# A fused long convolution and maxout feed-forward: where a hand-ordered kernel places its copies, folds and table loads

## The chip, the cores and the metric

The kernel runs on one core of a Trainium2 chip. The metric is the device time of one execution in microseconds (us), and the median over several executions is what is compared. Before the change it is 2282.52 us over 3 runs (2280.43 to 2288.77).

## The reference

A gated long convolution (batch 4, length 12544, 128 channels) feeds a maxout feed-forward layer (768 hidden units). Cut to what matters:

```python
h = (np.maximum(pos_emb @ w1, 0.0) @ w2) * np.exp(-0.01 * pos)[:, None]
u = x * v
y = irfft(rfft(u, n=2*S, axis=1) * rfft(h, n=2*S, axis=0)[None], n=2*S, axis=1)[:, :S]
t = (x * y).reshape(B * S, D)
out = np.maximum(np.maximum(t @ moe_w1, t @ moe_w2), t @ moe_w3) @ moe_w_out
```

All numbers are 32-bit floats.

## The kernel before

**Stages.** The transforms are done as matmuls on TensorE, in two steps: a first step of short transforms per block of four channels (a "unit" `u`, 32 per batch), and a second step per pair `g` of frequencies (45 pairs, `NK`). The filter's own transform and the whole convolution of batch 0 come first ("direct" stage, loop over `s` at L1072). After them comes a "passage" (L1106 to L1172), and then the main stage: for each batch the feed-forward runs over 32 tiles of 392 columns, and beside it, in the gaps that the feed-forward leaves on the other engines, the convolution of the next batch. The last batch's tiles have nothing beside them.

**Order.** The order of all instructions is written out by hand (L147); each engine takes its instructions in that order, and the waits between engines follow from the tiles. A tile in PSUM or SBUF is waited for as a whole. A pool with `bufs=2` gives out two buffers in turn, and the third request waits for the release of the first.

**The direct stage.** Step `s` multiplies pair `s` by the filter's second transform (`s_second`), forms the filter's spectrum of pair `s-1` (`s_filter`, copied to `ht` by ScalarE, L1050), and runs the inverse of pair `s-3` (`g_third`, L570, copied to `zs` by ScalarE and stored to `zd` in DRAM by SP). For pair `s-2` it stores `ht` to `hd` in DRAM from GpSimd's queue (`s_store`, L1054; later batches read it back), takes the complex product on VectorE (`g_re`, `g_im`: three instructions of about 0.69 us) and unfolds the result (`g_unfold`, two of 0.42). At step `NK` the pairs 43 and 44 are both due. At the steps `NK` and `NK + 1` stand units 0 and 1 of batch 1.

**A unit.** `u_first` (L404) does half a unit at a time: 16 matmuls (L413) into a PSUM bank, a copy `high` of one half of the result by ScalarE (L423), and a sum and a difference on VectorE into `spec` (L425). Its input `uT` is the transposed product x*v. Units up to 5 of batch 1 (`EARLY`) are transposed on TensorE (`u_turn`, L368). All later ones go another way: loads by SP (`u_load`), the product on GpSimd (`u_mul`, L361), a copy into two planes of 16-bit halves on ScalarE (`u_planes`, L382), a transposing DMA from SP (`u_dma`, L388), and `u_join` (L392), which puts the halves together again in two copies, L397: one on ScalarE, one on VectorE.

**The passage.** The third weight matrix times the output matrix is folded into one matrix `lin`: six times a transpose (L1007), a copy `w1t` on ScalarE (L1009) and a product accumulated in the bank `pl` (L1010). Units 4 and 5 of batch 1 are transposed between the folds. Then the pools of the first stages are closed. The main stage begins with the loads of two tiles of batch 0 (`t_load`, L675), the sums of the first on VectorE (`t_sums`, L701), unit 2, the tile's last transform (`t_last`, L717: 64 matmuls and a product `gt` on VectorE, L735), the sums of the second, unit 3, and then the loop over the tiles.

**The main loop.** A slot is one sixth of a tile. In each slot `up` (L740) makes two products of 128 hidden units in the banks `hps` (three in turn, L1137); ScalarE takes the first out with a ReLU into `hid` (L745), VectorE takes the maximum with the second (L748). The first eight tiles of a batch go in pairs with seven products instead of eight (`products`, L798), whose sums run on GpSimd (L778) and which need the weight differences `tw` and `linx`: five subtractions, L1190, in the first slots of batch 0.

**What runs beside, and when.** `conv_steps` (L582) plans the next batch's convolution by slot: the units first, then the pairs from slot `s0`. By its formulas `s0` is 55 for batch 1 and 59 for batches 2 and 3. Pairs are started two at a time, about 2.6 slots per pair. For pair `x` SP loads a table (`w_load`, L431, 256 KB, three buffers), for two pairs at a time the spectrum (`q_load`, L437, four transfers of 128 KB, two buffers) and the filter back from `hd` (`h_load`, L451, four transfers of 256 KB, two buffers). The buffers exist from slot `LOADS` = 52 on. SP's queue also carries the tiles' loads (`t_load`, L1198) and, up to that slot, stores of results. `g_quarter` (L462) uses the table and the spectrum in slot `start(x)`, `q_re` uses the filter three slots later or more.

Of the kernel before, what the change touches and what calls it, by code (L numbers as in the profile page):

```python
# [10 lines left out]
FP32 = mybir.dt.float32  # L11
# [5 lines left out]
P = 128  # L17
# [74 lines left out]
def kernel(  # L92
# [299 lines left out]
    def u_join(u):  # L392
        if u % 2 == 0:
            uts[u] = uts[u + 1] = utp.tile([NB, 16, 2, 32], FP32, tag="uT", name="uT")
        t = us.pop(u)
        for h in range(2):
            copies[h](  # L397
                uts[u][:, 8 * (u % 2):8 * (u % 2) + 8].rearrange(
                    "n s r t -> n (s r t)").bitcast(U16).rearrange(
                    "n (s r t h) -> n h s r t", h=2, r=2, t=32)[:, h],  # L400
                t[0:NB, 4 * h:4 * h + 4].rearrange("n s p -> n (s p)").rearrange(
                    "n (s t r) -> n s r t", s=8, r=2))

    def u_first(u, i0=0, n=4):  # L404


        t = uts[u] if i0 + n < 4 else uts.pop(u)
        ps = state["bank"]()[:, 0:256 * n]
        at = 4 * u + i0
        for i in range(n):  # L410
            for h in range(2):
                for c in range(2):
                    nc.tensor.matmul(  # L413
                        ps[64 * c:64 * c + 64, 256 * i + h * N1:256 * i + (h + 1) * N1],
                        t[:, 2 * ((at + i) % 8) + h].rearrange("n r t -> n (r t)"),
                        f1q[:, h, c * N1:(c + 1) * N1],
                        start=(i % 2 == 0 and h == 0), stop=True, skip_group_check=True)
        v = ps.rearrange("p (s m) -> p s m", m=256)[:, :, 0:2 * N1].rearrange(
            "p s (h k) -> p h k s", h=2)
        high = cvp.tile([P, state["eo"]], FP32, tag="eo", name="high", bufs=2)  # L420
        high = high[:].rearrange("p (s k) -> p s k", k=D)[:, 0:n, 0:N1].rearrange(
            "p s k -> p k s")
        nc.scalar.copy(high, v[:, 0])  # L423
        for a, op in enumerate((ALU.add, ALU.subtract)):
            nc.vector.tensor_tensor(out=spec[:, :, a, at:at + n], in0=v[:, 1], in1=high, op=op)  # L425

# [125 lines left out]
    def g_re(g):  # L552
        xt = xts[g]
        nc.vector.tensor_tensor(out=xt[:], in0=xt[:], in1=hts[g][:, 0], op=ALU.mult)
# [27 lines left out]
    def conv_steps(b, done):  # L582


        out = []

        def at(slot, late, fn, *args):
            out.append((slot, late, len(out), fn, args))

        for u in range(4, done):
            at(2 * (u - 4), 1, unit, u)
        lead, low = (1, -NT * NF) if b > 1 else (6, 0)
        share = UNIT * (NU - done - 1)
        per_pair = (END - lead - 6) / (share + (NK + LATE) // 2 * 2 - 2)
        for u in range(done, NU):
            s = (u - done) * UNIT * per_pair + lead
            load_ = max(low, int(s) - 9)
            at(load_, 0, u_load, b, u)  # L600
            mul = max(load_ + 2, int(s) - 6)
            at(mul, 0, u_mul, u, nc.gpsimd)
            at(max(mul, int(s) - 5), 0, u_planes, u)
            at(max(mul + 1, int(s) - 4), 0, u_dma, u)
            at(int(s), 0, u_join, u)
            at(int(s + 1), 1, unit, u)
        s0 = int(share * per_pair + lead) + 6

        def start(x):
            return s0 + int(x // 2 * 2 * per_pair)  # L610

        load = [0.6] * (NT * NF)
        for x in range(NK + LATE):
            s = start(x)
            load[s] -= 1.2
            load[s + 1 + x % 2] += 1.4

        def emptiest(among, cost):
            s = min(among, key=lambda i: load[i])
            load[s] += cost  # L620
            return s

        plan = []
        busy = {start(x): 2 for x in range(NK + LATE)}
        for x in range(NK + LATE):
            busy.setdefault(start(x) + 1, 1)
        for i in range(NT - 1):
            s = i * NF
            last = min((3, 4, 2), key=lambda k: busy.get(s + k, 0))
            load[s + last] += 0.6  # L630
            if s <= s0:
                plan.append((0, 0, last))
                continue
            a = emptiest(range(s, s + 2), 0.7) - s
            plan.append((a, emptiest(range(s + a, s + max(a + 1, last - 1)), 0.7) - s, last))
        plan.append((3, 3, 4))

        for x in range(NK + LATE):
            s, odd = start(x), x % 2
            g, z = x if x < NK else None, x - LATE if x >= LATE else None  # L640
            at(s, 1, g_quarter, g, z)
            at(s + 1 + odd, 0, g_fold, g, z)
            at(max(s - 4, LOADS), 0, w_load, x)
            if z is not None:
                at(s + 3 + odd, 0, g_store, b, z)
            if g is None:
                continue
            if g % 2 == 0:
                at(max(s - 4, LOADS), 0, q_load, g, min(2, NK - g))
                at(s - 1, 0, h_load, g, min(2, NK - g))  # L650
            first = s + 2 + 2 * odd
            at(first, 0, q_swap, g, 0)
            at(first + 1, 0, q_swap, g, 64)
            last = start(x + LATE) - 1
            a = emptiest(range(first + 1, min(first + 3, last - 1) + 1), 0.7)
            at(a, 0, q_re, g)
            a = emptiest(range(a, min(first + 4, last - 1) + 1), 0.7)
            at(a, 0, q_im, g)
            two = sorted(emptiest(range(a + 1, last + 1), 0.55) for _ in range(2))
            for q in range(2):  # L660
                at(two[q], 0, q_unfold, g, q)
        slots = {}
        for s, _, _, fn, args in sorted(out, key=lambda r: r[:3]):
            slots.setdefault(s, []).append((fn, args))
        return slots, plan, s0
# [332 lines left out]
    def bank():  # L998
        return next(free)

    state = {"cv": (cvp, cps), "xb": 2, "bank": bank, "eo": 2 * D,
             "turn": lambda: sps.tile([P, 512], FP32, tag="pl", name="pst")}
    Gs, minus = {}, {}

# [54 lines left out]

    EARLY = 6  # L1060
    loads = dict(zip((NK - 16, NK - 14, NK - 12, NK - 9, NK - 8, NK - 4), range(EARLY)))
    muls = dict(zip((NK - 13, NK - 11, NK - 10, NK - 5, NK - 3, NK - 1), range(EARLY)))
    turns = {NK - 9: 0, NK - 8: 1, NK - 4: 2, NK - 3: 3}
    folded = []

# [6 lines left out]
    for s in range(NK + 3):  # L1072
        if s < NK:
            ws[s, 0] = wf[s]
            s_second(s)
            if s + 1 < NK:
                s_minus(s + 1)
            g_second(s)
            wf.pop(s)
            if s + 3 < NK:  # L1080
                wf[s + 3] = load_dir(s + 3, 0)
        if 1 <= s <= NK:
            g_swap(s - 1)
            s_filter(s - 1)
        if s >= 3:
            ws[s - 3, 1] = wi.pop(s - 3)
            g_third(s - 3)
            if s < NK:
                wi[s] = load_dir(s, 1)
        for g in {NK: (s - 2, s - 1)}.get(s, (s - 2,)):  # L1090
            if 0 <= g < NK and s <= NK:
                s_store(g)
                g_re(g)
                g_im(g)
                g_unfold(g)
        if s < NK:
            g_butterfly(s)

        if s in muls:
            u_mul(muls[s])  # L1100
        if s in turns:
            u_turn(turns[s])
        if s in loads:
            u_load(1, loads[s])
        if s in (NK, NK + 1):
            unit(s - NK)  # L1106
    pl = sps.tile([P, 512], FP32, tag="pl", name="pl")
    state["turn"] = bank
    for f in range(NF):
        folding(f)  # L1110
        if f in (2, 3):
            u_turn(f + 2)
# [14 lines left out]
    b21, b22 = wo_sb[:, NC:, 0:64], wo_sb[:, NC:, 64:128]  # L1127
    weights = [(tw[:, 1], b22, b12), (tw[:, 3], b12, b11), (tw[:, 0], b22, tw[:, 3]),
               (tw[:, 2], b21, tw[:, 0]), (linx[:], lin[:, 0:64], lin[:, 64:128])]
    op_ = ctx.enter_context(tc.tile_pool(name="op", bufs=2))  # L1130
    conv = ExitStack()
    inq = conv.enter_context(tc.tile_pool(name="inq", bufs=1))
# [10 lines left out]
        turn_of["at"] = (turn_of["at"] + 1) % turn_of["of"]  # L1143
        return singles[turn_of["at"]]

    state = {"bank": single, "eo": 4 * D}
    sp = {"hid": ("h11",), "store": nc.sync}


# [9 lines left out]
    for n, (b, i) in enumerate(tiles[:LAST]):  # L1159
# [13 lines left out]
        for f in range(NF):  # L1173
            s = i * NF + f
            turn_ = i == NT - 1
            if i < TP:
# [8 lines left out]
                    down(*late.pop(0))  # L1185
                if n == 0 and f == 0:
                    t_last(tiles[1])
                elif weights:
                    out, a1, a2 = weights.pop(0)
                    nc.vector.tensor_tensor(out=out, in0=a1, in1=a2, op=ALU.subtract)  # L1190
                if j == 0:
                    banks = (obank, singles[3])
                    down_pair(b, i0, h, banks if i0 % 4 == 0 else banks[::-1], s, ends,
# [114 lines left out]
```

## Time and profile before

| what | before |
|---|---|
| median of 3 runs, us | 2282.52 (2280.43 to 2288.77) |
| the profiled execution, us | 2285.45 |
| span in its trace, us | 2283.7 |
| TensorE busy, us (share) | 2248.9 (98%) |
| VectorE busy, us (share) | 1554.7 (68%) |
| ScalarE busy, us (share) | 1264.1 (55%) |
| GpSimd busy, us (share) | 1010.7 (44%) |
| VectorE copies L397, number, mean ns | 90, 1015 |
| ScalarE copies L397, number, mean ns | 90, 777 |
| ScalarE copies `high` L423 from unit 2 of batch 1 on, number, mean ns | 188, 489 |

The names in the profile: PE is TensorE, PEld its weight loads, DVE VectorE, ACT ScalarE, POOL GpSimd, SP SyncE, a q behind a name the queue of that engine; L156 and the like are lines of the kernel, and L156 is that of a helper with which most matmuls are made, so its rows are told apart by their tiles (`hps` hidden units, `ops` output, `cps` with `f4p` a tile's last transform, `ps` with `ab` a pair's inverse). "a <- b" in a list of waits says that a stood idle until b had ended. The direct stage ends near 299 us, the main loop starts near 312, batch 2's convolution begins beside batch 1's tiles at 824, batch 3's near 1345.

### The profile page before, as it was taken

Reading aid. Unit: us, or ns where it says so; the run is one execution under the profiler, and the core shown is the slowest. Engines: PE = TensorE matmul, PEld = TensorE weight load, DVE = VectorE, ACT = ScalarE, POOL = GpSimd, SP = SyncE. Lnnn points to the kernel's source line nnn. Section 1 sums busy time; section 2 is a strip of 40 time slices with the busy share of each in tenths; the row PEclk is TensorE's granted clock in tenths of the full one; section 3 lists DMA queues with packets and bytes.
Section 4 is the critical chain, followed back from the end, with each engine's and each line's share of the span. In section 5 each row is a group of like instructions: output and inputs, shape, how many; then the busy total and the mean of one; then the engine's idle time right before and its main releaser. Section 6 shows DMA issues by size and latency. Waiting matters only on the chain.

```text
span 2283.7 us, 70396 instructions
## 1 busy us (share of the span) xinstructions
PE 2248.9 (98%) x28383; PEld 1427.1 (62%) x28383; DVE 1554.7 (68%) x3016; ACT 1264.1 (55%) x2308; POOL 1010.7 (44%) x1203
## 2 busy tenths in 40 slices
PE   8999989999999999999999999999999999999998
PEld 7988857755555557755555557765555556666665
DVE  5588967657878756658888856658888844544443
ACT  2688856556666656646666646646666622222222
POOL 2044447613333357713333347713333326666666
PEclk9999999999999999999999999999999999999999
DMA  7778989789999789969999889979999832222221
GB/s 187 183 231 269 305 179 179 135 199 248 228 241 234 199 165 186 167 149 250 251 239 233 228 158 182 170 148 254 252 238 232 215 85 56 56 68 67 59 56 22
DMA packets 485569, 411.17 MB, mean 180 GB/s; under 512 B 341305, under 2 KB 387866, under 8 KB 485242
## 3 DMA queue, kind: packets, MB, share of 16 engines
q1 hardware_dynamic: 459778, 334.30, 65.3%
q0 software_dynamic: 24752, 70.65, 10.4%
q8 instruction: 223, 3.65, 0.7%
q10 hardware_dynamic: 712, 1.70, 0.3%
q14 instruction: 104, 0.85, 0.1%
HBM read 262.84 MB, written 84.67 MB: 152 GB/s over the span
## 4 chain that ended last, share of the span: by engine, by line
PE 94%; DMA 3%; DVE 1%; POOL 1%; issue 1%; ACT 1%; SPq 0%; POOLq 0%; ACTq 0%; DVEq 0%
PE hps L156 43%; PE ops L156 14%; PE ops L809 8%; PE cps L413 5%; PE cps L156 4%; PE cps L472 3%; PE ps L156 3%; PE ps L165 3%; PE cps L482 3%; PE cps L809 2%; PE sps L1045 2%; PE gps L1027 1%; PE last L156 1%; DMA hd<-ht 1%; PE pst L366 1%; DMA wt<-wq_const 1%
## 5 line engine op out<-in xcount | busy, mean ns | idle before, releaser
L156 PE MATMUL hps<-gt,w_sb 128*64 128x392 f32 x6144 | 1150.6, 494 | 1.7 <-ACT hid L745 1.7
L745 ACT ACTIVATE hid<-hps 128x392 f32<-128x392 f32 x768 | 382.4, 498 | 665.9 <-PE hps L156 626.1
L156 PEld LDWEIGHTS hps<-gt,w_sb 128*64 128x64 f32 x6144 | 435.8, 137 | 406.0 <-issue 362.7
L748 DVE TENSOR_TENSOR hid<-hid,hps 128x392 f32<-128x392 f32 x768 | 428.5, 558 | 375.6 <-PE hps L156 340.0
L524 POOL TENSOR_TENSOR cb<-cb,xs 128x512 f32<-128x512 f32 x135 | 174.8, 1295 | 457.9 <-DVE xs L521 361.2
L156 PE MATMUL ops<-hid,wo_sb 128*64 128x392 f32 x1728 | 358.4, 492 | 0.0
L497 DVE TENSOR_TENSOR cb<-cps,eo 128x512 f32<-128x512 f32 (+1 forms) x288 | 175.1, 649 | 73.1 <-ACT eo L494 73.1
L156 PEld LDWEIGHTS ops<-hid,wo_sb 128*64 128x64 f32 x1728 | 125.7, 137 | 157.7 <-issue 157.7
L512 ACT ACTIVATE xs<-cb 32x512 f32<-32x512 f32 x270 | 169.5, 628 | 19.6 <-DVE cb L497 10.9
L763 POOL DMA_DIRECT2D out_dram<-ot x72 | 56.8, 789 | 275.4 <-ACT ot L761 223.8
L513 ACT COPY xs<-cb 32x512 f32<-32x512 f32 x270 | 166.3, 616 | 3.1
L425 DVE TENSOR_TENSOR spec<-cps,high 128x180 f32<-128x180 f32 x376 | 110.7, 339 | 69.8 <-ACT high L423 67.5
L423 ACT COPY high<-cps 128x180 f32<-128x180 f32 x188 | 90.9, 489 | 115.7 <-PE cps L413 79.9
L528 DVE TENSOR_TENSOR xs<-cb 128x256 f32<-128x256 f32 x270 | 143.8, 578 | 9.4 <-POOL cb L524 9.4
L413 PE MATMUL cps<-f1q,uT 98*64 98x90 f32 x3008 | 137.2, 243 | 6.3 <-DVE uT L397 5.9
L413 PEld LDWEIGHTS cps<-f1q,uT 98*64 98x64 f32 x3008 | 131.1, 138 | 15.3 <-issue 6.3
L778 POOL TENSOR_TENSOR s<-hid 128x392 f32<-128x392 f32 x84 | 87.2, 1038 | 89.5 <-DVE hid L748 56.1
L505 POOL DMA_DIRECT2D zd<-cb x135 | 92.7, 687 | 63.7 <-DVE cb L497 60.8
L156 PEld LDWEIGHTS cps<-f4p,even 90*64 90x64 f32 x1568 | 91.5, 138 | 30.6 <-issue 28.3
L778 POOL TENSOR_TENSOR s<-hid,s 128x392 f32<-128x392 f32 x84 | 87.3, 1040 | 51.6 <-DVE hid L748 51.3
L361 POOL TENSOR_TENSOR ut<-ut 128x392 f32<-128x392 f32 x90 | 94.9, 1054 | 34.1 <-DMA ut<-in_vr_dram 31.9
L778 POOL TENSOR_TENSOR hid<-hid,s 128x392 f32<-128x392 f32 x84 | 86.5, 1032 | 33.1 <-PE cps L809 9.6
(148 smaller groups left out, 3586.4 us busy)
## 6 DMA issues: line engine op xcount, KB each, us to landing
ht<-hd SPq DMA_DIRECT2D x264, 256.0 KB, 7.0
wt<-wq_const SPq DMA_DIRECT2D x144, 256.0 KB, 6.6
zd<-cb POOLq DMA_DIRECT2D x135, 256.0 KB, 6.2
zt<-zd SPq DMA_DIRECT2D x384, 90.0 KB, 3.2
sq<-spec SPq DMA_DIRECT2D x264, 128.0 KB, 7.2
ut<-in_xr_dram SPq DMA_DIRECT2D x128, 196.0 KB, 3.9
ut<-in_vr_dram SPq DMA_DIRECT2D x128, 196.0 KB, 4.2
xT<-in_x_dram SPq DMA_DIRECT2D x256, 98.0 KB, 3.5
```

The lines of the kernel that those rows point to most:

```text
L156: nc.tensor.matmul(out[64 * h:64 * h + 64], lhsT[:, 64 * h:64 * h + 64], rhs, start=start, stop=stop, skip_group_check=True)
L413: nc.tensor.matmul(ps[64 * c:64 * c + 64, 256 * i + h * N1:256 * i + (h + 1) * N1], t[:, 2 * ((at + i) % 8) + h].rearrange("n r t -> n (r ...
L425: nc.vector.tensor_tensor(out=spec[:, :, a, at:at + n], in0=v[:, 1], in1=high, op=op)
L497: nc.vector.tensor_tensor(out=cb[:, a, lo:hi], in0=ps[0][:, lo:hi], in1=eo[:, lo:hi], op=op)
L512: nc.scalar.mul(xs[at:at + 32], xt[at + 32:at + 64], -1.0)
L513: nc.scalar.copy(xs[at + 32:at + 64], xt[at:at + 32])
L524: nc.gpsimd.tensor_tensor(out=xts[g], in0=xts[g], in1=xs[:], op=ALU.add)
L528: nc.vector.tensor_tensor(out=ab[:, q], in0=y[:, 0], in1=y[:, 1], op=(ALU.subtract, ALU.add)[q])
L745: nc.scalar.activation(h[:], pa[:, 0:N], Relu)
L748: nc.vector.tensor_tensor(out=h[:], in0=h[:], in1=pb[:, 0:N], op=ALU.max)
L778: nc.gpsimd.tensor_tensor(out=out[:], in0=a[:], in1=b[:], op=op)
L809: nc.tensor.matmul(ps[64 * c:64 * c + 64, 0:H2], w, rhs[:, H2 * c:H2 * c + H2], start=start, stop=True, skip_group_check=True)
```

## The change

It has five parts.

- `u_join`: both copies L397 on ScalarE.
- `u_first`: the engine of `high` is given by the stage: ScalarE in the direct stage and the passage, VectorE in the main loop.
- The passage. At step `NK + 1` the first two folds stand in place of unit 1, and unit 1 comes after the last step, ahead of the other four folds; the bank `pl` is taken at step `NK`. At step `NK` the unfolds of pairs 43 and 44 follow the products of both, and pair 43's last sum goes to GpSimd. The product x*v of unit 5 moves from step `NK - 1` to step `NK`.
- The five weight differences go from VectorE's first slots to GpSimd, ahead of the main loop.
- The loads of the first pairs: the tables of pairs 0 and 1 in slot 52, that of pair 2 in slot 53, the filter of pairs 0 and 1 in slot 53 and of pairs 2 and 3 in slot 54. Before, the tables were loaded four slots ahead of their pair (not before slot 52) and the filter one slot ahead.

```diff
--- before.py
+++ after.py
@@ -394,7 +394,7 @@
             uts[u] = uts[u + 1] = utp.tile([NB, 16, 2, 32], FP32, tag="uT", name="uT")
         t = us.pop(u)
         for h in range(2):
-            copies[h](
+            nc.scalar.copy(
                 uts[u][:, 8 * (u % 2):8 * (u % 2) + 8].rearrange(
                     "n s r t -> n (s r t)").bitcast(U16).rearrange(
                     "n (s r t h) -> n h s r t", h=2, r=2, t=32)[:, h],
@@ -420,7 +420,7 @@
         high = cvp.tile([P, state["eo"]], FP32, tag="eo", name="high", bufs=2)
         high = high[:].rearrange("p (s k) -> p s k", k=D)[:, 0:n, 0:N1].rearrange(
             "p s k -> p k s")
-        nc.scalar.copy(high, v[:, 0])
+        state["high"](high, v[:, 0])
         for a, op in enumerate((ALU.add, ALU.subtract)):
             nc.vector.tensor_tensor(out=spec[:, :, a, at:at + n], in0=v[:, 1], in1=high, op=op)
 
@@ -640,14 +640,14 @@
             g, z = x if x < NK else None, x - LATE if x >= LATE else None
             at(s, 1, g_quarter, g, z)
             at(s + 1 + odd, 0, g_fold, g, z)
-            at(max(s - 4, LOADS), 0, w_load, x)
+            at(max(s - 4, LOADS) if x > 2 else LOADS + x // 2, 0, w_load, x)
             if z is not None:
                 at(s + 3 + odd, 0, g_store, b, z)
             if g is None:
                 continue
             if g % 2 == 0:
                 at(max(s - 4, LOADS), 0, q_load, g, min(2, NK - g))
-                at(s - 1, 0, h_load, g, min(2, NK - g))
+                at(s - 1 if g > 2 else LOADS + 1 + g // 2, 0, h_load, g, min(2, NK - g))
             first = s + 2 + 2 * odd
             at(first, 0, q_swap, g, 0)
             at(first + 1, 0, q_swap, g, 64)
@@ -998,7 +998,7 @@
     def bank():
         return next(free)
 
-    state = {"cv": (cvp, cps), "xb": 2, "bank": bank, "eo": 2 * D,
+    state = {"cv": (cvp, cps), "xb": 2, "bank": bank, "eo": 2 * D, "high": nc.scalar.copy,
              "turn": lambda: sps.tile([P, 512], FP32, tag="pl", name="pst")}
     Gs, minus = {}, {}
 
@@ -1059,7 +1059,7 @@
 
     EARLY = 6
     loads = dict(zip((NK - 16, NK - 14, NK - 12, NK - 9, NK - 8, NK - 4), range(EARLY)))
-    muls = dict(zip((NK - 13, NK - 11, NK - 10, NK - 5, NK - 3, NK - 1), range(EARLY)))
+    muls = dict(zip((NK - 13, NK - 11, NK - 10, NK - 5, NK - 3, NK), range(EARLY)))
     turns = {NK - 9: 0, NK - 8: 1, NK - 4: 2, NK - 3: 3}
     folded = []
 
@@ -1087,12 +1087,13 @@
             g_third(s - 3)
             if s < NK:
                 wi[s] = load_dir(s, 1)
-        for g in {NK: (s - 2, s - 1)}.get(s, (s - 2,)):
-            if 0 <= g < NK and s <= NK:
-                s_store(g)
-                g_re(g)
-                g_im(g)
-                g_unfold(g)
+        ready = [g for g in {NK: (s - 2, s - 1)}.get(s, (s - 2,)) if 0 <= g and s <= NK]
+        for g in ready:
+            s_store(g)
+            g_re(g)
+            g_im(g, g == NK - 2)
+        for g in ready:
+            g_unfold(g)
         if s < NK:
             g_butterfly(s)
 
@@ -1102,11 +1103,15 @@
             u_turn(turns[s])
         if s in loads:
             u_load(1, loads[s])
-        if s in (NK, NK + 1):
-            unit(s - NK)
-    pl = sps.tile([P, 512], FP32, tag="pl", name="pl")
+        if s == NK:
+            unit(0)
+            pl = sps.tile([P, 512], FP32, tag="pl", name="pl")
+        if s == NK + 1:
+            for f in range(2):
+                folding(f)
+    unit(1)
     state["turn"] = bank
-    for f in range(NF):
+    for f in range(2, NF):
         folding(f)
         if f in (2, 3):
             u_turn(f + 2)
@@ -1127,6 +1132,8 @@
     b21, b22 = wo_sb[:, NC:, 0:64], wo_sb[:, NC:, 64:128]
     weights = [(tw[:, 1], b22, b12), (tw[:, 3], b12, b11), (tw[:, 0], b22, tw[:, 3]),
                (tw[:, 2], b21, tw[:, 0]), (linx[:], lin[:, 0:64], lin[:, 64:128])]
+    for out, a1, a2 in weights:
+        nc.gpsimd.tensor_tensor(out=out, in0=a1, in1=a2, op=ALU.subtract)
     op_ = ctx.enter_context(tc.tile_pool(name="op", bufs=2))
     conv = ExitStack()
     inq = conv.enter_context(tc.tile_pool(name="inq", bufs=1))
@@ -1143,7 +1150,7 @@
         turn_of["at"] = (turn_of["at"] + 1) % turn_of["of"]
         return singles[turn_of["at"]]
 
-    state = {"bank": single, "eo": 4 * D}
+    state = {"bank": single, "eo": 4 * D, "high": nc.vector.tensor_copy}
     sp = {"hid": ("h11",), "store": nc.sync}
 
 
@@ -1185,9 +1192,6 @@
                     down(*late.pop(0))
                 if n == 0 and f == 0:
                     t_last(tiles[1])
-                elif weights:
-                    out, a1, a2 = weights.pop(0)
-                    nc.vector.tensor_tensor(out=out, in0=a1, in1=a2, op=ALU.subtract)
                 if j == 0:
                     banks = (obank, singles[3])
                     down_pair(b, i0, h, banks if i0 % 4 == 0 else banks[::-1], s, ends,
```

## The prediction

> **What bounds the kernel now.** I read the page first (busy shares and chain), then the waits of TensorE, then the timeline of each place where TensorE stands still, engine by engine.
>
> ```profile
> PE 2248.9 (98%) x28383; PEld 1427.1 (62%) x28383; DVE 1554.7 (68%) x3016; ACT 1264.1 (55%) x2308; POOL 1010.7 (44%) x1203
> ...
> PE 94%; DMA 3%; DVE 1%; POOL 1%; issue 1%; ACT 1%; SPq 0%; POOLq 0%; ACTq 0%; DVEq 0%
> ```
>
> TensorE is busy 2248.9 of 2283.7 us and is 94% of the chain. The diff takes no matmul away, so all it can win lies in the 34.8 us in which TensorE stands still (added up in the timeline, the gaps make about 26). Their owners, columns total us, times, longest us:
>
> ```profile
> PE cps L413 <- DVE uT L397: 5.9, 6, 1.8
> PE ps L413 <- DVE spec L425: 3.6, 1, 3.6
> ...
> PE cps L472 <- DMA wt<-wq_const: 2.1, 2, 1.6
> PE hps L156 <- ACT hid L745: 1.7, 2, 1.4
> PE cps L156 <- DVE even L710: 1.5, 1, 1.5
> ```
>
> The diff aims at the first three and the last: 13.1 us, 0.57% of the time. About 7 us more lie at the start of the kernel, which it doesn't touch. The passage, in the chain of waits (start, us, what):
>
> ```profile
> 285.85 5.89 DMA hd<-ht
> ...
> 291.84 1.02 ACT ht L1050
> ...
> 292.89 0.69 DVE xt L554
> ...
> 295.01 0.76 DVE ab L566 x2
> ...
> 297.64 0.84 PE ps L413 x16
> 298.48 0.89 PE ps L156 x16
> ...
> 300.00 2.16 DMA zd<-zs
> ...
> 303.29 3.69 DMA zt<-zd
> ```
>
> The reader sees a latency chain: pair 44's filter copy (`ht`) waits for a store to land, the last pair's products follow on VectorE, then its inverse (L156), and from there 9.3 us pass over DRAM until the first tile of batch 0 can start at 307.84. TensorE's work in between only has to fit.
>
> **What the Trainium skill says.** "SBUF — State Buffer", section "SBUF: two separate sides": VectorE and GpSimd share a port pair as an exclusive lock; a VectorE copy in a 2-port mode, or an operation with two SBUF inputs, is blocked for a whole GpSimd instruction, ScalarE never. The trace agrees for the join (L397):
>
> ```profile
> 833.45 2.85 DVE L397 COPY uT<-turned 98x512 uint16<-98x512 uint16 x1
> ```
>
> The same copy takes 0.45 us on VectorE at 830.53, its mean is 1.015, and ScalarE takes 0.777 every time. "TensorE: Matmul & The Clock Gate", section "What's actually happening": a free-running window of 3413 ns with too little matmul halves the clock for about as long. The windows of 1 us show one such fall (PEclk is the third column from the right):
>
> ```profile
> 309.00:310.00 1.00, 1.00 (x30) 1.00 (x28) 0.89 (x4) 0.00 (x0) 0.00 (x0) 0.74 0.56 172
> 310.00:311.00 1.00, 1.00 (x18) 1.00 (x16) 0.77 (x2) 0.13 (x1) 0.00 (x0) 0.50 0.06 18
> 311.00:312.00 1.00, 1.00 (x16) 1.00 (x14) 0.97 (x3) 0.35 (x1) 0.00 (x0) 0.50 0.59 160
> ```
>
> About 3.4 us at half clock cost 1.7 us of matmul, right after the idle stretch of 306.3 to 308.6.
>
> **Joins to ScalarE, upper halves to VectorE.** VectorE loses 90 joins x 1.015 = 91.4 us and gains 188 copies 128x180 out of PSUM. The trace has no such copy on VectorE: not under 0.19 us (the 0.339 of L425 with its second operand free would hardly be less), not over the 0.489 that ScalarE takes; I take 0.30, the start-to-start time of L425 in its runs of four (1.2 us), so 56 us. ScalarE gains 90 x 0.777 = 70 and loses 188 x 0.489 = 92 us. Both engines get lighter. What stands in order: behind the double join (1.55 us) on ScalarE wait the planes' copy and the next `hid` (L745). I replayed ScalarE's rows of the three stretches with units (330 to 456, 828 to 990, 1346 to 1507), second join added, `high` taken out: `hid` starts up to 0.77 us later in about 50 of 153 places, and TensorE wants its bank back never less than 0.13 us after it ends, mostly 1.2. So this costs nothing; if that cover were gone, 50 x some 0.3 = 15 us. The six waits are at 329.8 (0.53), 399.3 (0.35), 433.6 (1.22), 834.7 (1.78), 868.1 (0.23), 1352.8 (1.78). At 834.7 the two joins would run 832.83 to 834.4, ahead of TensorE's 834.67. I count the last five, **-5.4 us**, bounds -6 and -2. `high` on VectorE shortens the hop from matmul to spectrum; nothing waits for that now.
>
> **The passage.** Removed: the wait of 3.58 us ahead of unit 1's second half (it shares a PSUM tile with the first, so it waits for L425, which was queued behind pair 44's products). But the new loop puts both unfolds behind both pairs' products. Pair 44's first product can't start before `ht` ends at 292.86; products and sum take to 294.9, unfold 43 (0.76) to 295.7. Inverse 43, which started at 292.35, now starts at 295.7: **a new wait of 3.4 us takes the old one's place.** Pair 43's sum on GpSimd (1.295 us by the row of L524) is done before, hidden under the wait for `ht`; so is the later product of unit data 5 (0.56). Then fold transposes to 297.0, the copy of inverse 43 (0.59) and of the first fold (0.27) to 297.8, a fold product, inverse 44 at 298.1 (now 298.28). From there the DRAM chain is the same: the first tile at 307.7 instead of 307.84. In the 9.6 us fit unit 1 (1.5, with a new wait of some 1.25 between its halves), four folds and two turns (some 4) and unit 2 (1.5): they end at about 307.1. So: -0.15. Then VectorE: `high` of unit 2 (2 x 0.3) now stands behind the tile's sums, which wait for the DMA, so the first `gt` comes at 310.8 instead of 310.2. Without the half clock (the window before is now full) TensorE is there 0.9 earlier than the 311.77 of now; from 318 GpSimd's row of sums and products (busy without a gap to 340) leads, and starts 0.4 earlier. I count **-0.5** for the passage. Ends: -2.5 if TensorE, not GpSimd, leads; +1.5 if the new 3.4 us wait falls into one window and halves the clock under inverse 43 and 44.
>
> **Weight differences to GpSimd.** Five instructions leave VectorE (3.1 us, 317.9 to 327.7) for GpSimd, which stands idle before 318.12 for 23.93 us. They wait for `lin` (304.8) and, at some 0.5 to 1.0 us each, are done by 310. **0**; if they ended after 318 they would delay the chain there by what is over.
>
> **Tables loaded ahead.** SP issues in order, and its issues go eight deep: at 478.43 the table of pair 3 is issued as the eighth transfer before it lands (`ht` of 472.90 lands at 478.36).
>
> ```profile
> 478.36 0.02 issue
> ...
> 478.43 7.89 DMA wt<-wq_const
> ...
> 486.37 0.67 PE cps L472 x16
> ```
>
> That is TensorE's wait of 0.50 us in batch 1; batch 2 has one of 1.58 (1012.7), batch 3 none. In **batch 1** the diff takes `h_load(2)`, four issues, from slot 59 to slot 54, which is ahead of `q_load(2)` and of the table of pair 3. `w_load(2)` was ahead of them anyway. Going through the eight-deep queue by hand, the last `sq` is issued at 480.1 instead of 477.2 and the table at 480.7 instead of 478.43, and lands at 487.3 to 488.6: the wait grows from 0.5 to 1.4 to 2.7, **+1.6**. In **batch 2** SP waits 4.5 us for the last unit's L425 ahead of `q_load(0)`. Tables 0 to 2 and both filters now go ahead of that wait, so six transfers fewer stand between `q_load(0)` and the table of pair 3 (12, now 18): **-1.6**. But ten go ahead of `q_load(0)`: 15 transfers from 981.03 instead of 5, its last issue 992 instead of 991.1, and with 7.2 us to landing that meets TensorE's 999.3. **+0.5** for batches 2 and 3 together (0 to 4). Sum **+0.5**, ends -2 and +6.
>
> **Sum.** -5.4 - 0.5 + 0 + 0.5 = -5.4 us. The profiled execution took 2285.45 (span 2283.7 and 1.75 around it) and would take 2280.1. It lay 2.9 over the median 2282.52 of the runs (2280.43 to 2288.77), so the median to be expected is 2277.1. What a measurement of this kernel can tell from no change is about 0.5%, 11.4 us: below 2271.1 or above 2293.9.
>
> **Rivals.** (1) **The queue on SP turns the end slower.** The loads ahead push the spectrum's transfers back: batch 1 pays 4 x 0.8 = 3.2 us, batches 2 and 3 2 us each ahead of the first pair, and each stop halves the clock for a window (1.7 each): 12.3, less the 1.6 of batch 2, for my 0.5. Total +4.8: 2287. It decides from where `q_load(0)`'s last issue comes later than about 992, and outweighs the joins from 6 us of new stops. For it: the eight-deep issue at 478. Against: stops of 1.78 us have left the clock at 1.00. (2) **The joins' wait only changes hands:** two copies in a row on ScalarE, with `hid` and planes before them, leave some 0.8 of each wait. 2281.5. For it: the first units of a batch have little lead; against: the replay. (3) **The passage and the queue both give:** `ht` comes earlier, inverse 44 moves to 296, the half clock goes, batch 1 pays nothing: -4.5 and -1.6 more, 2271.5. Against: the store that `ht` waits for is untouched.
>
> **Chances.** Forecast 0.60, (1) 0.15, (2) 0.12, (3) 0.13. The forecast's own range is 2272 to 2282; to 8 in 10 it takes most of (1) and (3): 2269 to 2288. Faster by over 0.5% is the far half of (3), slower the far end of (1): 0.08 and 0.08.
>
> **What would show it.** Right: no wait of L413 for `uT`; L397 all on ScalarE at 0.78; a wait of some 3.4 us of L156 for `ab` near 292.3; clock 1.00 at 309 to 313; the wait at 1012.7 gone, that at 486 larger. Wrong: inverse 43 still at 292.4, new waits of `hps` for `hid`, of L472 for `sq` over 2 us, or a half clock after them.

## The result, and the profile after

The change made the kernel slower by 0.3%. Over 13 runs each, the kernel before has a median of 2288.77 us (2280.43 to 2291.22) and the changed one 2294.16 (2288.35 to 2298.61); the ratio is 1.0029, 95% interval 1.0016 to 1.0042. The forecast was 2277.1, 0.24% faster. The three runs of before that it was built on lay low among the thirteen, so the ratio is what compares: on 2282.52 it gives 2289.1, past the 2288 at which the prediction's wider range ends.

The page of the changed kernel (span 2288.5, the execution itself 2290.28), the lines that answer to those shown of before:

```profile
PE 2254.5 (99%) x28383; PEld 1397.2 (61%) x28383; DVE 1545.8 (68%) x3108; ACT 1227.9 (54%) x2210; POOL 1004.3 (44%) x1209
...
PE 94%; DMA 3%; issue 1%; SPq 1%; POOL 0%; ACT 0%; DVE 0%; POOLq 0%; ACTq 0%; DVEq 0%
```

TensorE has the same 28383 matmuls and is busy 5.6 us longer: part of the loss is no wait at all, but slower matmuls. TensorE's waits in the changed kernel:

```profile
PE cps L472 <- DMA sq<-spec: 7.9, 7, 3.0
PE ps L156 <- DVE ab L566: 4.3, 1, 4.3
...
PE hps L156 <- ACT hid L745: 1.9, 2, 1.0
PE ps L413 <- DVE spec L425: 1.3, 1, 1.3
PE cps L413 <- ACT uT L397: 1.2, 2, 0.6
```

The wait for `uT` has gone from 5.9 to 1.2 us, as meant. New are 7.9 us for `sq`, the spectrum of the first pairs, and 4.3 us for `ab` in the passage. The first happens in all three batches. Batch 1, TensorE's timeline (start, us, and in brackets the idle time before):

```profile
482.09 0.83 PE L156 MATMUL ops<-hid,wo_sb 128*64 128x392 f32 x4
485.90 0.43 PE L472 MATMUL cps<-sq,wt 64*64 64x128 f32 x4 [2.99 <-DMA sq<-spec]
487.28 2.24 PE L472 MATMUL cps<-sq,wt 64*64 64x128 f32 x28 [0.94 <-DMA sq<-spec]
489.29 1.08 PE L482 MATMUL cps<-xs,wt 64*64 64x128 f32 x16
490.30 2.23 PE L156 MATMUL hps<-gt,w_sb 128*64 128x392 f32 x6
```

Behind a stop of 3.9 us in two pieces, the first six matmuls of a hidden unit take 2.23 us; before, eight took 1.5. The windows of 1 us of the same kernel say why (PEclk is the third column from the right):

```profile
486.00:487.00 1.00, 0.34 (x4) 0.09 (x3) 0.06 (x1) 0.00 (x0) 0.81 (x1) 0.90 1.10 181
487.00:488.00 1.00, 0.72 (x12) 0.75 (x12) 0.00 (x0) 0.00 (x0) 0.45 (x1) 0.50 1.10 172
488.00:489.00 1.00, 1.00 (x16) 0.61 (x16) 0.00 (x0) 0.00 (x0) 0.00 (x0) 0.50 1.24 197
```

The clock stayed at half for 6.8 us from 486.8 on, which costs 3.4 us of matmul. In batch 3 a stop of 1.4 and 0.5 us is followed by 3.4 us at half clock. The stop comes from SP's queue. There, first in the kernel before (with the matmuls that read this spectrum), then in the changed one:

```profile
474.79 3.16 SPq L443 DMA_DIRECT2D sq<-spec  x4
478.43 0.34 SPq L433 DMA_DIRECT2D wt<-wq_const  x1
479.73 3.35 SPq L456 DMA_DIRECT2D ht<-hd  x4
...
485.20 0.67 PE L472 MATMUL cps<-sq,wt 64*64 64x128 f32 x16
```

```profile
472.09 3.03 SPq L456 DMA_DIRECT2D ht<-hd  x4
476.14 3.30 SPq L443 DMA_DIRECT2D sq<-spec  x4
480.30 0.34 SPq L433 DMA_DIRECT2D wt<-wq_const  x1
```

The four filter transfers (L456) that stood behind pair 3's table before now stand ahead of the spectrum. TensorE asks for that spectrum at 482.92; its last transfer is issued at 478.93 and lands at 487.14. In the kernel before the last one was issued at 477.44, 8 us ahead of the demand (485.20), and landed some 0.1 us ahead of it: there was no slack to spend. In the changed kernel it is issued 4 us ahead. What held it, in the chain of waits (start, us, what), is the landing of the transfer eight places before it, the tile's second `zt`:

```profile
471.19 7.73 DMA zt<-zd
478.92 0.02 issue
478.93 8.21 DMA sq<-spec
```

### The profile page after: what moved, and what is told of

It reads as the page before. It is cut to its first block, busy times and chain, and to the rows that moved or that the text cites. A ratio compares the mean times of both kernels' runs of the same rounds, so it can differ in the third digit from the quotient of the medians.

```text
span 2288.5 us, 70172 instructions
## 1 busy us (share of the span) xinstructions
PE 2254.5 (99%) x28383; PEld 1397.2 (61%) x28383; DVE 1545.8 (68%) x3108; ACT 1227.9 (54%) x2210; POOL 1004.3 (44%) x1209
## 4 chain that ended last, share of the span: by engine, by line
PE 94%; DMA 3%; issue 1%; SPq 1%; POOL 0%; ACT 0%; DVE 0%; POOLq 0%; ACTq 0%; DVEq 0%
PE hps L156 43%; PE ops L156 14%; PE ops L809 8%; PE cps L413 5%; PE ps L156 4%; PE cps L156 4%; PE cps L472 3%; PE ps L165 3%; PE cps L482 3%; PE cps L809 2%; PE sps L1045 2%; PE gps L1027 2%; PE last L156 1%; DMA zt<-zd 1%; DMA sq<-spec 1%
## 5 line engine op out<-in xcount | busy, mean ns | idle before, releaser
L745 ACT ACTIVATE hid<-hps 128x392 f32<-128x392 f32 x768 | 382.2, 498 | 822.5 <-PE hps L156 794.6
L156 PEld LDWEIGHTS hps<-gt,w_sb 128*64 128x64 f32 x6144 | 419.9, 137 | 420.3 <-issue 387.1
L397 ACT COPY uT<-turned 98x512 uint16<-98x512 uint16 x180 | 127.5, 781 | 0.0
L423 DVE COPY high<-cps 128x180 f32<-128x180 f32 x188 | 89.9, 478 | 23.2 <-PE cps L413 21.8
```

Of the source, the lines that this page charges most:

```text
L156: nc.tensor.matmul(out[64 * h:64 * h + 64], lhsT[:, 64 * h:64 * h + 64], rhs, start=start, stop=stop, skip_group_check=True)
L397: nc.scalar.copy(uts[u][:, 8 * (u % 2):8 * (u % 2) + 8].rearrange("n s r t -> n (s r t)").bitcast(U16).rearrange("n (s r t h) -> n h s r t ...
L745: nc.scalar.activation(h[:], pa[:, 0:N], Relu)
```

## The experiments

Three theories stood against each other at first: that the loads ahead hold up the spectrum in SP's queue (Q, rival 1 of the prediction), that the exchange of joins and upper halves costs the time (J), or that the passage does (P). The first four runs undo or do one part alone. Each ratio is to the kernel before, of which 18 to 52 executions were measured beside each group of runs; of the kernels themselves there are 6 to 22 executions. Waits and stretches are read from one profiled execution of each.

**Loads as before.** The changed kernel, with

```diff
-            at(max(s - 4, LOADS) if x > 2 else LOADS + x // 2, 0, w_load, x)
+            at(max(s - 4, LOADS), 0, w_load, x)
...
-                at(s - 1 if g > 2 else LOADS + 1 + g // 2, 0, h_load, g, min(2, NK - g))
+                at(s - 1, 0, h_load, g, min(2, NK - g))
```

> The changed kernel with one part undone: the tables and filters of the first pairs are loaded in their old slots. Theory Q (the loads ahead push the spectrum's transfers back in SP's queue): the waits of L472 for sq at the first pairs (3.0 + 0.9 in batch 1, 1.7 in batch 2, 1.4 + 0.5 in batch 3) and the half clocks after them go, the old waits for the table (0.5 and 1.6) come back; 5.5 us of waits and some 5 us of half clock less, so 8 to 10 us faster than the changed kernel and 2 to 4 us faster than the one before: ratio about 0.9985. Theory J (the exchange of joins and upper halves costs the time in the main loop): the time stays near the changed kernel's, ratio 1.002 to 1.003. Theory P (the passage with its new wait and half clock costs it): likewise 1.002 or more.

Measured: ratio 0.9978 (0.9968 to 0.9987), no wait for `sq` over 0.3 us, waits for the table of 1.25, 1.52 and 0.61 us, and no half clock after the passage. The rest of the change is a gain; undoing the loads took 0.5% off.

**Loads only.** The kernel before with the same two lines changed the other way.

> The kernel before with only the loads of the first pairs put ahead. Theory Q: waits of L472 for sq of 1 to 3 us in each of the three batches, a half clock in at least one, 8 to 10 us slower: ratio 1.0035 to 1.0045. Theories J and P: no change beyond 0.1%.

Measured: 1.0056 (1.0036 to 1.0077), some 13 us slower (8 to 18 over the interval; seven executions), more than expected. Waits in its trace:

```profile
PE cps L472 <- DMA sq<-spec: 9.3, 6, 4.0
PE cps L413 <- DVE uT L397: 8.6, 7, 2.5
```

The stop of 4.0 us is batch 2's first pair, with a half clock behind it, and batch 1 has stops of 2.4, 0.8 and 0.4 us (the last for a table) and a half clock. Theory Q holds in both directions. Not all that this profile lost comes from the loads: in the first slots of batch 0, ahead of them, it has a stop of 3.7 us for ScalarE's `hid` with a half clock of 6.8 us.

**The exchange only.** The kernel before with both joins on ScalarE and `high` on VectorE from unit 2 on:

```diff
-            copies[h](
+            nc.scalar.copy(
...
-        nc.scalar.copy(high, v[:, 0])
+        state["high"](high, v[:, 0])
```

> The kernel before with only the exchange: both joins on ScalarE, upper halves on VectorE from unit 2 on. Theory Q, with the exchange as forecast: the six waits of L413 for uT fall from 5.9 to about 1.2 us and nothing takes their place: 4 to 5 us faster, ratio 0.998. Theory J: new short waits in the units' stretches, 3 us or more slower, ratio 1.001 or more.

Measured: 0.9983 (0.9975 to 0.9991), 3.9 us faster; the waits for `uT` are down to two of 0.6 us, at the first unit of batches 2 and 3. J is out. One thing was not expected: new waits of `hps` for VectorE's `hid`, 1.0 and 2.95 us, near 326 and 328. VectorE's timeline there:

```profile
323.62 2.21 DVE L1190 TENSOR_TENSOR tw<-wo_sb,tw 128x192 f32<-128x192 f32 x1
325.76 0.55 DVE L748 TENSOR_TENSOR hid<-hid,hps 128x392 f32<-128x392 f32 x1
326.23 4.09 DVE L1190 TENSOR_TENSOR tw<-wo_sb,tw 128x192 f32<-128x192 f32 x1
```

These two weight differences took 0.35 and 0.70 us in the profile of before, and take 2.2 and 4.1 here beside GpSimd's sums. Each has two operands in SBUF, and that is the case in which the Trainium skill ("SBUF — State Buffer", "SBUF: two separate sides") lets a GpSimd instruction block VectorE; 4.09 us is longer than any one GpSimd instruction there (at most 1.3). The exchange is not needed for it: in the profile of the run with the loads only the second of them takes 4.5 us as well.

```profile
326.69 4.46 DVE L1190 TENSOR_TENSOR tw<-wo_sb,tw 128x192 f32<-128x192 f32 x1
```

So where they stood, the weight differences cost TensorE up to 4 us in some executions (here) and next to nothing in others (before).

**The passage only.** The kernel before with the rearranged steps `NK` and `NK + 1`, and the weight differences left on VectorE.

> The kernel before with only the passage rearranged (folds in place of unit 1, unfolds behind both products, pair 43's sum on GpSimd), weight differences where they were, on VectorE. Theory Q with the passage as read from the trace: a wait of L156 for ab of 3.4 us near 289 to 292, without the 0.9 us that GpSimd's weight differences added in the changed kernel; a half clock behind it; the main loop's first slots 1 to 2 us later than before: ratio 1.0005 to 1.001. Theory P: 3 us or more, ratio 1.0015 or more.

Measured: 1.0002 (0.9989 to 1.0015): no change that can be told. The wait for `ab` is there, with 1.96 us, 1.4 below the forecast. The time from the start of pair 44's `ht` to the eighth `hid` of the main loop is 37.6 us in the profile of before, 41.9 here, and 41.5 in the run with the loads only, whose passage is untouched: half clocks of 3.4 to 17 us in all fall into the passage and the first slots in every profile, not always at the same place, and cover a difference of 2 us. By the interval (up to 3.4 us slower) P is out as the main cost.

The next four ask what in the loads costs, and test the two side effects.

**Tables ahead only.** The changed kernel with `h_load` alone back in its old slot.

> The changed kernel with only the filters (h_load) back in their old slots; the tables of pairs 0 to 2 stay ahead. Theory F (the eight filter transfers of 256 KB, put ahead of the spectrum in SP's queue, are the cost): the waits of L472 for sq fall below 0.5 us in all three batches, no half clock after them, time near that of the kernel with all loads as before: ratio 0.9975 to 0.9985. Theory W (the tables, or the number of transfers whatever they are): waits for sq of 1 us or more stay in batches 2 and 3, ratio 1.000 or more.

Measured: 0.9967 (0.9955 to 0.998). No wait for `sq` is left in the trace and one of 0.20 us for a table, in batch 1:

```profile
483.41 0.67 PE L472 MATMUL cps<-sq,wt 64*64 64x128 f32 x16
484.28 0.67 PE L472 MATMUL cps<-sq,wt 64*64 64x128 f32 x16 [0.20 <-DMA wt<-wq_const]
```

So the tables ahead are harmless, and by the trace a gain: the waits for tables, 1.25, 1.52 and 0.61 us with all loads as before, are gone but for this. In time the two runs' intervals overlap.

**Filters behind the spectrum.** The filters three slots ahead of their pair instead of one, but behind `q_load`:

```diff
-                at(s - 1 if g > 2 else LOADS + 1 + g // 2, 0, h_load, g, min(2, NK - g))
+                at(s - 1 if g > 2 else max(s - 3, LOADS + 1), 0, h_load, g, min(2, NK - g))
```

> The changed kernel with the filters of the first pairs still loaded earlier than before, but behind the spectrum of their pairs in SP's queue (three slots ahead of the pair in place of slots 53 and 54). Theory F by order (only what stands ahead of q_load and of the third pair's table counts): no wait for sq above 0.5 us, ratio 0.9975 to 0.9985. If it is the mere earlier traffic that counts: waits for sq of 1 us or more stay, ratio 1.000 or more.

Measured: 0.9969 (0.9956 to 0.9983), no wait for `sq` over 0.15 us. The run tells less than it was meant to. In SP's queue its order differs from that of the run before, tables ahead only, in one place: in batch 1 the filter of pairs 0 and 1 goes ahead of a table and of the tile's `zt`. In batches 2 and 3 the filters stand where they stood. So this one early filter does no harm; whether the same traffic, as early as in the changed kernel but behind the spectrum, would cost less is not shown. What is shown is that the filters moved ahead of the spectrum are the cost, and the tables are not. Three stretches of the main loop, from one `hid` to another (L745, counted from 0), in us of each profile:

| hid | before | changed | loads as before | loads only | tables only | filters behind | stops filled |
|---|---|---|---|---|---|---|---|
| 43 to 66 (batch 1) | 69.9 | 75.4 | 69.8 | 74.2 | 67.7 | 67.7 | 73.0 |
| 248 to 262 (batch 2) | 39.1 | 39.7 | 39.0 | 43.7 | 37.3 | 37.3 | 41.1 |
| 440 to 455 (batch 3) | 39.3 | 43.3 | 40.3 | 41.4 | 39.3 | 39.3 | 42.2 |

The changed kernel loses 9.2 us in them against the one with loads as before (158.3 to 149.2), which is most of what the ratios say (0.51%, 11.7 us). The loads only lose 11.1 against the kernel before.

**Weight differences behind lin.** The changed kernel with loads as before and one more line, so that GpSimd waits for `lin` first:

```diff
-    for out, a1, a2 in weights:
+    for out, a1, a2 in weights[-1:] + weights[:-1]:
```

> The changed kernel with all loads as before and the weight differences on GpSimd in another order: linx first, which needs lin, so that the other four run after the folds and not beside pair 44's product. Theory S (GpSimd's subtractions with two SBUF operands at 290.9 to 293.7 hold up VectorE's sum and unfolds): VectorE's L559 and L566 back to 0.69 and 1.5 us together 2 us sooner, the wait of L156 for ab 2.0 to 2.4 in place of 4.3; the time up to 2 us less than with the loads as before alone (0.9978), or the same, if the DRAM chain to the first tile sets the end. Rival: L559 stays at 1.7 us and the wait at 4.3.

Measured: 0.9956 (0.9939 to 0.9972), against 0.9978 (0.9968 to 0.9987) without the line; the intervals overlap. VectorE in the passage, first in the changed kernel (columns start, us), then in this one:

```profile
290.82 1.73 DVE L559 TENSOR_TENSOR xt<-xt,xs 128x512 f32<-128x512 f32 x1
292.47 2.20 DVE L566 TENSOR_TENSOR ab<-xt 128x256 f32<-128x256 f32 x4
```

```profile
290.56 0.69 DVE L559 TENSOR_TENSOR xt<-xt,xs 128x512 f32<-128x512 f32 x1
291.17 1.42 DVE L566 TENSOR_TENSOR ab<-xt 128x256 f32<-128x256 f32 x4
```

Sum and unfolds take 2.0 us instead of 3.9, and the wait for `ab` is 1.8 instead of 4.3 (4.4 with the loads as before). What ran beside them in the changed kernel, on GpSimd:

```profile
290.85 1.14 POOL L1136 TENSOR_TENSOR tw<-wo_sb 128x192 f32<-128x192 f32 x2
292.06 1.66 POOL L1136 TENSOR_TENSOR tw<-wo_sb,tw 128x192 f32<-128x192 f32 x2
```

Theory S holds, and the other profiles say the same. Inverse 44 starts 8.5 us after the start of pair 44's `ht` in each of the five kernels whose weight differences run at this place, 6.0 in the three that have the new passage without them there (passage only, this one, and tables and weights below), and 6.4 to 7.0 in the three with the old passage. The first tile's sums (L710) start 18.0 to 18.3, 15.7 to 16.0, and 15.3 to 16.7 us after it. So the weight differences lengthen this chain by some 2.5 us, and without them the new passage is no slower than the old one up to the first tile. The wait for `ab` by itself says less: it also moves by up to 1.1 us with the time at which `ht` comes, seen from unit 0.

**Stops filled.** The changed kernel with matmuls of no use ahead of the late pairs, to keep TensorE occupied while it waits.

```diff
+        if g == 0:
+            quarters.append(g)
+        if (len(quarters), g) in ((1, 2), (2, 0), (3, 0)):
+            for _ in range(4 if g else 2):
+                halves_mm(ps[0][:, 0:N], w_sb[2][:, 0:P], w_sb[1][:, 0:N], True, True)
```

> The changed kernel with matmuls of no use in the stops ahead of the late pairs (batch 1 pair 2: 16 records, 2.6 us; batches 2 and 3 pair 0: 8 records, 1.3 us), written to a bank that is overwritten; the output is the reference's. Theory C (part of the cost is the half clock that follows the stop): the half clock near 487 to 494 and near 1521 goes, the pairs come at the same time as in the changed kernel, and the time is 3 to 5 us less: ratio 1.0010 to 1.0015. Rival (the clock falls for another reason, or the extra matmuls lengthen the stop): same time as the changed kernel or more, 1.003 and up.

Measured: 1.0021 (1.0006 to 1.0036), between expectation and rival. The half clocks behind the pairs are gone; the windows of this kernel across the same pair of batch 1:

```profile
490.00:492.00 2.00, 0.81 (x8) 0.24 (x5) 0.89 (x2) 0.00 (x0) 0.98 (x1) 1.00 1.03 234
492.00:494.00 2.00, 1.60 (x44) 1.29 (x44) 0.00 (x0) 0.00 (x0) 0.28 (x1) 1.00 1.21 199
494.00:496.00 2.00, 2.00 (x20) 0.92 (x14) 0.26 (x1) 0.50 (x1) 0.00 (x0) 1.00 1.17 252
```

Batch 1's stretch is 2.4 us shorter than in the changed kernel, batch 3's 1.1, but batch 2's, which had no half clock to lose, is 1.4 longer. That the halved clock is part of the cost is shown in the trace; the gain in time, 0.0008 of the ratio, is within the intervals, so it is not shown.

The last two put the repairs together.

**Tables and weights.** Filters in their old slots, tables ahead, `linx` first.

> The changed kernel with the filters (h_load) in their old slots, the tables ahead, and linx first among GpSimd's weight differences. If the two costs found (filters ahead of the spectrum, weight differences beside pair 44's product) are separate, their repairs add: the tables ahead gave 0.9967, the weights behind lin 0.9956 with old loads; together no wait for sq or table over 0.5 us and a wait for ab of about 2 us: ratio 0.994 to 0.996. If they overlap: 0.9965.

Measured: 0.9963 (0.9949 to 0.9977); waits for tables and spectrum are 0.7 us at most. The wait for `ab` is 2.9 us, not the 2 expected, though VectorE is not held up (sum and unfolds 2.0 us): seen from unit 0, `ht` came 1.0 us later than in weight differences behind lin. The two repairs don't add beyond what either gave: 0.9967 and 0.9956 lie inside the interval, so how far they overlap stays open.

**Unfold 43 first.** The same kernel with

```diff
-            g_im(g, g == NK - 2)
-        for g in ready:
-            g_unfold(g)
+            g_im(g)
+            g_unfold(g)
```

> The kernel of e9 with one more edit: pair 43's sum back on VectorE and its unfold ahead of pair 44's product, as in the kernel before, with folds in place of unit 1 kept. Theory U (the wait of L156 for ab comes from the unfolds' place behind both products): that wait falls below 0.5 us, inverse 44 comes 1 to 2 us sooner after pair 44's ht, and the main loop starts up to 2 us sooner: ratio 0.0005 below e9's. Rival (the chain through DRAM or the half clock takes it back): same ratio as e9 within its interval.

Measured: 0.9947 (0.9928 to 0.9966), median 2277.13. TensorE's timeline in the passage of this kernel:

```profile
291.77 1.41 PE L413 MATMUL ps<-f1q,uT 98*64 98x90 f32 x32
293.19 1.09 PE L156 MATMUL ps<-ab,wt 128*64 128x128 f32 x16
294.22 0.44 PE L1007 MATMUL pt<-eye,w_sb 128*128 128x128 f32 x2
295.53 0.44 PE L156 MATMUL pl<-wo_sb,w1t 128*64 128x128 f32 x4 [0.87 <-ACT w1t L1009]
296.37 1.17 PE L156 MATMUL ps<-ab,wt 128*64 128x128 f32 x16 [0.41 <-issue]
```

Inverse 43 (293.19) follows unit 0 without a wait, inverse 44 starts 3.7 us after the start of pair 44's `ht` (292.68), against 6.0 in tables and weights and 8.5 in the changed kernel (296.99 after 288.44), and the first `hid` comes 19.9 us after it, against 21.4 and 23.9. So the order of the unfolds makes the wait for `ab`, and the weight differences lengthen it. In time, the intervals of this run (six executions) and of tables and weights overlap. It beats the kernel before by 0.5% and, ratio by ratio, the changed one by 0.8%.

## Why the prediction was wrong, point by point

- **Tables loaded ahead: +0.5 was the step that failed.** Against the loads as before, this part, by its filters and not its tables, was worth 9.2 us in the stretches of the profile (+5.6, +0.7 and +2.9 in batches 1 to 3) and 11.7 by the ratios. The mechanism, transfers put ahead of `q_load` in a queue whose issues go eight deep, was described in the prediction for each batch, and rival 1, with 12.3 us for it and +4.8 in all, named it as the way to a slower kernel; in the forecast two sizes were wrong.
  - The stops. TensorE waited 7.9 us for `sq`, where the kernel with loads as before waits 3.7 for tables and spectrum: 4.2 more, not 0.5. In batch 1 the working let the last `sq` be issued 3 us later and priced only the wait for pair 3's table behind it, 1.4 to 2.7; the stop was 3.9, for the spectrum, which had had 0.1 us to spare. In batch 2 the last `sq` was issued at 997.7 for a demand at 1001.4, 3.7 us ahead; the working had 992 for 999.3. The tile's `zt` between the filters landed after 6.5 to 9.2 us there (3.2 to 3.9 before), and each late landing holds the issue eight places behind. Batches 2 and 3 stopped for 1.9 us each instead of 0.5 together. Batch 2's old wait of 1.58 us did go.
  - The half clocks behind the stops, which the forecast put at nothing: 3.4 us of matmul in batch 1, 1.7 in batch 3. With the 4.2 us of stops they make up the 9.2.
- **"Stops of 1.78 us have left the clock at 1.00"** was the argument against rival 1's price, and it failed. It was true of those stops and says nothing of one of 3.9 us. A stop of 1.7 and 0.2 us in batch 2 of the changed kernel had no half clock behind it, 1.4 and 0.5 in batch 3 had one. The free-running window, of which the Trainium skill tells ("TensorE: Matmul & The Clock Gate", "What's actually happening"), agrees with that: in the clock records of every profile (but for the one that the end of the kernel cuts off) half clocks start whole multiples of 3.413 us apart and last 3.413 us or a multiple. On this grid batch 3's stop lies in one window, which leaves TensorE 46% busy; batch 2's is split over two, 77 and 67% busy. So in this kernel it mattered how much of one window a stop took, and not its length alone.
- **Joins and upper halves: -5.4.** Right in sign and mechanism; -3.9 by the ratio of the run with this alone (-2.1 to -5.7 over its interval). Two waits of 0.6 us remained, and the profiled execution of this run paid near 4 us for the weight differences on VectorE. The copy `high` on VectorE takes 0.478 us, near the upper bound given (0.489) and not the 0.30 taken; nothing waited for it.
- **Weight differences: 0 was wrong.** "They wait for `lin`" holds for the last of the five only. The other four ran at 290.85, in the middle of pair 44's product, and blocked VectorE: inverse 44 came 2.5 us later after `ht`. The prediction had quoted the rule of the shared port, and applied it to the joins alone.
- **The passage: -0.5.** No difference is measured (1.0002). The wait in front of inverse 43 came where it was forecast: 4.3 us in the changed kernel, 1.8 to 2.9 without the weight differences beside it, instead of 3.4. The half clock near 310 went, but others came, at 292.3 to 299.1 under inverses 43 and 44, which is the case that the prediction priced at +1.5, and at 302.5 to 305.9.

The parts add up within the intervals: loads +12.8, exchange -3.9, passage +0.5 from the runs with one part alone make +9.4 us; the change measured +6.6. No run moves the weight differences alone, so what they are worth in the whole is not known, and the interval of the loads by itself (8 to 18 us) is wider than the difference of 3.

## What to carry to other kernels

A load moved ahead in a queue that issues in order is a load put in front of others: ask what is next in that queue, when TensorE wants it, how much slack it has now, and count the landing times with the added traffic, not those of the quiet profile. If a stop of TensorE grows to some 2 us or more, count with a halved clock behind it, here 1.7 or 3.4 us of matmul. An instruction moved to GpSimd runs as soon as its operands and its place in GpSimd's order allow, so look at what VectorE does at that moment, and give it a dependence that keeps it away. And before a control run is read, compare its order of instructions with that of its neighbour: here one change of slots left the queue almost as it had been.

## What the runs showed of the hardware

- A VectorE subtraction with two operands in SBUF (128x192) took 0.35 us with GpSimd idle, and 4.09 and 4.46 us in two profiles beside an unbroken row of GpSimd instructions of 0.3 to 1.4 us: longer than any one of them, so it seems to be blocked several times in a row. The join's copy of 2.85 us that the prediction shows had instructions of at most 1.3 us beside it, too. A VectorE sum of 128x512 took 0.69 us alone and 1.73 beside GpSimd's subtractions.
- A copy 128x180 out of PSUM takes 0.478 us on VectorE and 0.489 on ScalarE, while a sum of the same shape with one operand in PSUM takes 0.34 on VectorE.
- SP's transfers go eight deep: when the queue is full, an issue starts 0.02 to 0.07 us after the landing of the transfer eight places before it (478.93 after 478.92).
- Half clocks in the main loop follow the busy share of a window on the grid of 3.413 us. In the twelve profiles six windows at full clock were followed by one, with TensorE 13 to 46% busy; ten with 48 to 58% were not, nor was one with 45%. Busy shares rest on modelled ends of matmuls, and in the passage, with its small matmuls, a window of 63% was followed by a half clock, so this is no general threshold.
- The same stretch with the passage untouched, from pair 44's `ht` to the eighth `hid`, took 37.6, 39.9 and 41.5 us in three profiles. The longer two have the slow subtraction above, the longest a half clock of 6.8 us in the first slots besides.
